# A recurrent attention kernel with streamed weights: 35 resident halves instead of 34, one shared work region, a new order of the step, and longer rows for streamed query and key halves

## The chip, the cores and the metric

The kernel runs on one core of a Trainium2 chip. The metric is the device time of one execution in microseconds, as the median of several runs. Engines are named as the profile names them: TensorE (PE; its weight loads are PEld), VectorE (DVE), ScalarE (ACT), GpSimd (POOL), and SyncE (SP), which here issues nearly all DMAs.

## The reference

The sequence has 2048 rows of 640 in bfloat16. Four residual sublayers follow one another: A, B, A, B, each on the layer norm of its input. Both layers use the same weights.

```python
# A: recurrent attention with a memory of 8 rows, 32 heads of 192, segments of 32 rows
for s in range(64):
    h = concatenate([mem, xs])                  # 8 + 32 rows
    q, k, v = h @ Wq, h @ Wk, h @ Wv            # each 640 x (32*192)
    p = softmax(where(mask, q @ k.T * scale, -1e9))
    o = (p @ v) @ Wo                            # (32*192) x 640
    mem, out_s = o[:8], o[8:]

# B: local attention, 32 heads of 20, each row sees 8 rows at distance 0, 2, ... 14 behind it
q, k, v = split(x @ wqkv)
o = softmax(q . k_window * scale) . v_window
out = o @ wo

x = x + A(layernorm(x)); x = x + B(layernorm(x))
x = x + A(layernorm(x)); x = x + B(layernorm(x))
```

The memory makes A a chain of 64 dependent segments. Its four weight matrices have 31.5 MB together, more than fits on the chip.

## The kernel before, in words

**Steps.** The kernel works in 67 steps, numbered 0 to 66. Step s runs A for segment s of layer 0 and for segment s - 2 of layer 1 (`LAG = 2`), stacked into one set of operands `ST` so that each weight is loaded once for both, and B for the segments that the step before finished. Step 66 has only B's part.

**Halves.** The four matrices of A are cut into 64 "halves" of 128 x 1920 elements (480 KB each): 0 to 31 are key and query halves (even and odd), 32 to 47 are V, 48 to 63 are output. 34 of them stay resident on the chip. The other 30 (`STREAMED`) come anew in every step, through a ring of five buffers `wt`. In step 0 a streamed half is loaded from the input and also written, in the layout of the ring, to a scratch tensor `Wr` in HBM; from step 1 on it comes from there, in two transfers of 240 KB (`half`). A ring buffer comes free when TensorE has done the last matmul of the half five places earlier.

**Order.** A hand-written list, `ORDER`, says in which order the parts of a step are issued. TensorE, VectorE, ScalarE and SP keep that order exactly; GpSimd's is chosen by the scheduler. The names that the text uses:

- q0 to q15: keys and queries of a pair of heads, 30 matmuls from two halves; ScalarE copies the result (`QK`). s0 to s3, exp0 to exp3, soft0 to soft3: scores of a group, their exponentials on ScalarE, and their normalisation on VectorE (`Pm`). t0 to t3: transposes of the probabilities, which VectorE copies to `PT`.
- va, vb, vc: the values of a group, copied to `V` by ScalarE, or by VectorE for what `V_ON_VECTOR` lists (two copies for each va or vb). pv0 to pv3: probabilities times values, copied by ScalarE to `ot`. o0 to o14: output projection, 15 matmuls from one half (o14 takes the last two), summed over the step in `acc`.
- sqr, stat, root, norm, qkv, prod, logits, explg, attn, e0 to e4, wo: layer norm and local attention of B. prod multiplies queries with the key window, layer 0 on VectorE and layer 1 on GpSimd; the latter is issued in qkv. e0 to e4 expand the weights on TensorE, and VectorE multiplies and sums them.
- sqx, statx, rootx, normx: layer norm of B's result, for layer 1's next segment. store: every fourth step, 128 finished rows are transposed, copied by ScalarE to `yo` and sent out from ScalarE's queue.
- xs, xr, xn, xt, xw: every fourth step, 128 new input rows are normalised (xs, xr, xn) and transposed (xt); xw transposes the rows themselves. alpha puts one segment of them into the next step's `ST`.

Before the change, the input rows `x_sb` are loaded at the head of each step with s % 4 = 1 (`input_load`), xs to xt run in the step after, and xw in the step with s % 4 = 0. `yo` and the normalised rows `xn` take turns in one buffer (tag `xn`). `prod`, `x_sb`, `xn`/`yo` and the layer norm's float32 scratch (tag `f32n`) have buffers of their own.

Of the kernel before, what the change touches and what calls it, by code (L numbers as in the profile page):

```python
# [10 lines left out]
BF16 = mybir.dt.bfloat16  # L11
F32 = mybir.dt.float32
ACT = mybir.ActivationFunctionType
ALU = mybir.AluOpType
# [8 lines left out]
P = 128  # L23
# [31 lines left out]
N_HALVES = 64  # L55
N_RESIDENT = 34
RING = 5


ORDER = """  # L60
q0 sqr0 q1 xs0 stat0 root0 xr0 q2 q3 q4 s0 exp0 norm0 va0 vb0 vc0 qkv0 q5 soft0 t0 q6 q7 prod0 pv0
va1 vb1 vc1 logits0 s1 explg0 exp1 o0 attn0 o1 q8 q9 q10 alpha0 o2 soft1 t1 e0 q11 q12 s2 e1 o3 exp2
e2 q13 q14 pv1 va2 vb2 vc2 soft2 e3 t2 q15 o4 e4 o5 s3 pv2 exp3 va3 soft3 vb3 vc3 o6 o7 wo0 t3 o8
xw0 xn0 o9 sqx0 o10 store0 pv3 o11 xt0 statx0 o12 o13 rootx0 normx0 o14
"""


def stages():
# [8 lines left out]
PLAN = stages()  # L77
V_ON_VECTOR = (("va", 1), ("vb", 1),)


STREAMED = (
    0, 3, 5, 6, 9, 11, 12, 13, 14, 16, 19, 21, 22, 24, 26, 29, 32, 35, 37, 41, 42, 46, 47, 48, 52, 53, 55, 57, 59,
    61,
)
# [11 lines left out]

def window1(ap, c):

    v = ap[:, c, :, 0:SEG]
    dims = [list(x) for x in v.ap]  # L100
    return bass.AP(v.tensor, v.offset, dims[:2] + [[BDIL, BW]] + dims[2:])
# [22 lines left out]
class Kernel:  # L124
# [21 lines left out]
    def constants(self):  # L146
# [10 lines left out]
        nc.vector.memset(self.zero, 0.0)  # L157
        m1 = self.w1.tile([P, LT], F32, name="mask1", tag="f32n")
        nc.gpsimd.memset(m1[:], 0.0)
        for u in range(2):  # L160
            r = slice(SLOT * u, SLOT * (u + 1))
            nc.gpsimd.affine_select(out=m1[r, :], in_=m1[r, :], compare_op=ALU.is_ge, fill=NEG, base=0,
                                    pattern=[[-1, LT]], channel_multiplier=1)
            nc.gpsimd.memset(m1[SLOT * u:SLOT * u + NM, :], 0.0)
        self.maskA = cp.tile([P, LT], BF16, name="maskA")
        nc.vector.tensor_copy(out=self.maskA[:, :], in_=m1[:, :])

        self.E = cp.tile([P, NCH, BH], BF16, name="E")
# [27 lines left out]
        self.wo = cp.tile([P, NCH, D], BF16, name="wo")  # L196

        self.kh = cp.tile([P, NCH, 2, BPAD + SEG], BF16, name="kh")
        self.vh = cp.tile([P, NCH, 2, BPAD + SEG], BF16, name="vh")
# [12 lines left out]
        nc.vector.tensor_reduce(out=self.maskL, in_=pairs, op=ALU.max, axis=AX.X)  # L212
        m_sb = self.w1.tile([NM, D], BF16, name="m_sb", tag="xn")
        nc.sync.dma_start(out=m_sb[:, :], in_=self.mem0)
        mt = self.ps.tile([P, NCH, NM], BF16, name="mt", tag="ps")
# [20 lines left out]
    def half(self, h):  # L236
        if h in self.resident:
            return self.resident[h]
        if h in RESIDENT:
            t = self.res.tile([P, HALF], BF16, name=f"res{h}")  # L240
            self.load_direct(t, h)
            self.resident[h] = t
            return t
        t = self.ring.tile([P, HALF], BF16, name="wt")
        if self.step == 0:
            self.load_direct(t, h)
            self.nc.gpsimd.dma_start(out=self.Wr[h][:, :], in_=t[:, :])
        else:
            for part in (slice(0, HALF // 2), slice(HALF // 2, HALF)):
                self.nc.sync.dma_start(out=t[:, part], in_=self.Wr[h][:, part])  # L250
        return t
# [7 lines left out]
    def input_load(self, t):  # L259
        self.x_sb = self.w1.tile([P, D], BF16, name="x_sb")  # L260
        self.nc.sync.dma_start(out=self.x_sb[:, :], in_=self.x[t * P:(t + 1) * P, :])

# [13 lines left out]
    def input_norm(self, t):  # L276
        nc = self.nc
        x_sb, st = self.x_sb, self.x_st
        nc.vector.scalar_tensor_tensor(out=st[:, 3:4], in0=st[:, 0:1], scalar=-1.0, in1=st[:, 2:3], op0=ALU.mult, op1=ALU.mult)
        xn = self.w1.tile([P, D], BF16, name="xn", tag="xn")  # L280
        nc.vector.tensor_scalar(out=xn[:, :], in0=x_sb[:, :], scalar1=st[:, 2:3], scalar2=st[:, 3:4], op0=ALU.mult, op1=ALU.add)
        self.x_n = xn

# [21 lines left out]
    def ln_square(self, src, n):  # L305
        nc = self.nc
        sq = self.w1.tile([P, NCH, n], F32, name="sq", tag="f32n")
        nc.gpsimd.tensor_tensor(out=sq[:, :, :], in0=src, in1=src, op=ALU.mult)
        ssq = self.w1.tile([P, n], F32, name="ssq", tag="ssq")
        nc.vector.tensor_reduce(out=ssq[:, :], in_=sq[:, :, :].rearrange("p c n -> p n c"), op=ALU.add, axis=AX.X)  # L310
        return ssq

    def ln_stats(self, src, ssq, n):
# [9 lines left out]
        nc.vector.scalar_tensor_tensor(out=r[:, :], in0=ps[:, 1, :], scalar=1.0 / D, in1=r[:, :], op0=ALU.mult, op1=ALU.subtract)  # L323
        xc = self.w1.tile([P, NCH, n], F32, name="xc", tag="f32n")
        nc.vector.tensor_tensor(out=xc[:, :, :], in0=src, in1=m[:, :].unsqueeze(1).to_broadcast([P, NCH, n]), op=ALU.subtract)
        return xc, r
# [163 lines left out]
    def b_square(self):  # L490
        self.ssq_b = self.ln_square(self.rows_of_b(), 2 * SEG)

    def b_stats(self):
        self.ln_b = self.ln_stats(self.rows_of_b(), self.ssq_b, 2 * SEG)
# [8 lines left out]
    def b_qkv(self):  # L503
# [13 lines left out]
        self.qT = qT  # L517
        self.prod = self.w1.tile([P, NCH, 2, BW, SEG], BF16, name="prod")
        self.products(1, nc.gpsimd)

# [4 lines left out]
    def b_logits(self):  # L525
# [3 lines left out]
        for c in range(NCH):  # L529
            for r in range(4):  # L530
                nc.tensor.matmul(ps[32 * r:32 * (r + 1), :, :], lhsT=self.E[:, c, :], rhs=self.prod[:, c, r // 2, :, hf * (r % 2):hf * (r % 2 + 1)],
                                 start=(c == 0), stop=(c == NCH - 1), tile_position=(0, 32 * r))
# [28 lines left out]
    def b_expand(self, c):  # L561
        nc = self.nc
        ps = self.ps.tile([P, 2, BW, SEG], F32, name="bc_ps", tag="ps")
        nc.tensor.matmul(ps[:, :, :, :].rearrange("p l w t -> p (l w t)"), lhsT=self.ET[:, c, :],  # L564
                         rhs=self.attn[:, :, :, :, :].rearrange("p l w h t -> p (l w h t)"), start=True, stop=True)
        pv = self.prod[:, c, :, :, :]
        nc.vector.tensor_tensor(out=pv, in0=ps[:, :, :, :], in1=window1(self.vh, c), op=ALU.mult)  # L567
        with nc.allow_low_precision("bf16 result of an f32 sum"):
            nc.vector.tensor_reduce(out=self.oT[:, c, :].rearrange("p (l t) -> p l t", l=2), in_=pv.rearrange("p l w t -> p l t w"), op=ALU.add, axis=AX.X)  # L569

    def b_wo(self):
        nc, s = self.nc, self.step
        ps = self.ps.tile([P, NCH, 2, SEG], F32, name="y_ps", tag="ps")
        for d in range(NCH):
            for c in range(NCH):
                nc.tensor.matmul(ps[:, d, :, :].rearrange("p l t -> p (l t)"), lhsT=self.wo[:, c, d * P:(d + 1) * P], rhs=self.oT[:, c, :],  # L576
                                 start=(c == 0), stop=(c == NCH - 1))
# [27 lines left out]
    def store(self):  # L605
        nc = self.nc
        k = self.step - 1 - LAG
        if k < 0 or k % 4 != 3:
            return
        ps = self.ps.tile([P, NCH, P], BF16, name="yt_ps", tag="ps")  # L610
        for c in range(NCH):
            nc.tensor.transpose(out=ps[:, c, :], in_=self.yT[:, c, :], identity=self.ident[:, :])
        yo = self.w1.tile([P, D], BF16, name="yo", tag="xn")
        nc.scalar.copy(out=yo[:, :], in_=ps[:, :, :].rearrange("p c d -> p (c d)"))
        nc.scalar.dma_start(out=self.out[(k // 4) * P:(k // 4 + 1) * P, :], in_=yo[:, :])


    def run(self):
# [5 lines left out]
        with tc.manual_schedule(engines={PE, SP, VECTOR, SCALAR}):  # L624
# [11 lines left out]
            local = {"sqr": self.b_square, "stat": self.b_stats, "root": self.b_root, "norm": self.b_norm, "qkv": self.b_qkv,  # L636
                     "prod": lambda: self.products(0, nc.vector), "logits": self.b_logits, "explg": self.b_exps, "attn": self.b_soft, "wo": self.b_wo,
                     "sqx": self.beta_square, "statx": self.beta_stats, "rootx": self.beta_root, "normx": self.beta_norm, "store": self.store}
            rows_in = {"xs": self.input_stats, "xr": self.input_root, "xn": self.input_norm, "xt": self.input_turn}
            for s in range(n_steps + 1):  # L640
# [7 lines left out]
                self.x2 = self.x2_next  # L648
                if s % 4 == 1 and 4 * (s // 4 + 1) < self.n_seg:
                    self.input_load(s // 4 + 1)  # L650
                for what, i in PLAN:
# [6 lines left out]
                    elif what == "alpha" and a and s + 1 < self.n_seg:  # L658
                        self.alpha_x(s + 1)
                    elif what in rows_in and s % 4 == 2 and 4 * (s // 4 + 1) < self.n_seg:  # L660
                        rows_in[what](s // 4 + 1)
# [59 lines left out]
```

## Time and profile before

| | |
|---|---|
| median of 3 runs | 3428.22 us (3424.91 to 3428.84) |
| the profiled execution | 3421.51 us, span 3419.7 us |
| TensorE, matmuls | 3225.9 us busy, 94% of the span |
| VectorE, ScalarE, GpSimd | 2323.2, 1969.7 and 338.5 us busy |
| DMA | 1025.24 MB, mean 300 GB/s |
| chain that ended last | PE 81%, DMA 11%, DVE 3% |

The span is the time from the first to the last instruction in the profiled execution. A busy TensorE is not TensorE at its peak, because the ends of matmuls are modelled and consecutive ones overlap; the distance between the starts of matmuls tells more. In the tables of waits each row names the engine and line that waited, what released it, the total in us, the number of times and the longest.

### The profile page before, as it was taken

The numbers are of one execution on the slowest core, as the hardware profiler recorded it, in microseconds if no ns is written. First come the engines' busy times: TensorE is split into PE (matmuls) and PEld (weight loads), VectorE is DVE, ScalarE is ACT, GpSimd is POOL, SyncE is SP. The second block draws the span as 40 slices with busy tenths as digits, with TensorE's granted clock in tenths as the row PEclk, the third lists the DMA queues.
The fourth block names the chain that finished last, engine by engine and source line by source line (L and its number), as shares of the span: only waits on it lengthen the run. The fifth ranks groups of instructions, "written<-read, shape, count | busy, mean of one in ns | idle before, by whom it ended". The sixth has DMA issues, their size and how long they took to land.

```text
span 3419.7 us, 184327 instructions
## 1 busy us (share of the span) xinstructions
PE 3225.9 (94%) x83325; PEld 2782.4 (81%) x83325; DVE 2323.2 (68%) x5322; ACT 1969.7 (58%) x4269; POOL 338.5 (10%) x456
## 2 busy tenths in 40 slices
PE   4799999999999999999999999999999999999997
PEld 3588888888888888888888888888888888888886
DVE  1367767766776766776677677767767766776775
ACT  1365665656555565565655556565565656556564
POOL 2101010000101001010100100100010010001000
PEclk7799999999999999999999999999999999999998
DMA  9999999998999989989988999998999989899995
GB/s 347 356 299 299 304 301 301 301 305 295 299 303 295 298 289 305 304 296 309 302 296 293 301 297 301 308 299 292 301 300 302 305 298 303 292 308 303 305 297 182
DMA packets 608612, 1025.24 MB, mean 300 GB/s; under 512 B 64456, under 2 KB 605264, under 8 KB 607824
## 3 DMA queue, kind: packets, MB, share of 16 engines
q1 hardware_dynamic: 603120, 996.08, 87.9%
q8 instruction: 651, 10.67, 1.3%
q0 software_dynamic: 2400, 14.75, 1.1%
q10 hardware_dynamic: 2304, 2.62, 0.2%
q14 instruction: 137, 1.12, 0.1%
HBM read 995.83 MB, written 17.37 MB: 296 GB/s over the span
## 4 chain that ended last, share of the span: by engine, by line
PE 81%; DMA 11%; DVE 3%; issue 2%; SPq 2%; ACT 1%; ACTq 0%; POOLq 0%; POOL 0%; DVEq 0%
PE qk_ps L345 26%; PE acc L458 15%; PE v_ps L409 12%; DMA wt<-Wr 8%; PE v_ps L428 7%; PE o_ps L441 4%; PE qkv_ps L514 3%; PE s_ps L357 3%; PE bc_ps L564 2%; PE s_ps L363 2%; PE qk_ps L340 1%; PE y_ps L576 1%; PE pt_ps L395 1%; SPq L250 1%; SPq L234 1%
## 5 line engine op out<-in xcount | busy, mean ns | idle before, releaser
L347 ACT CAST QK<-qk_ps 128x480 bf16<-128x480 f32 x1056 | 585.7, 560 | 648.6 <-PE qk_ps L345 481.6
L419 ACT CAST V<-v_ps 32x384 bf16<-32x384 f32 (+1 forms) x1848 | 849.7, 470 | 181.9 <-PE v_ps L428 128.4
L345 PE MATMUL qk_ps<-ST,wt 128*128 128x80 bf16 x14850 | 685.3, 203 | 49.8 <-DMA wt<-Wr 22.3
L345 PE MATMUL qk_ps<-ST,res 128*128 128x80 bf16 x14850 | 664.9, 203 | 20.8 <-issue 7.9
L345 PEld LDWEIGHTS <-wt 128*128 128x128 bf16 x14850 | 601.6, 101 | 79.4 <-DMA wt<-Wr 29.8
L345 PEld LDWEIGHTS <-res 128*128 128x128 bf16 x14850 | 590.2, 101 | 27.5 <-issue 13.2
L397 DVE TENSOR_SCALAR PT<-pt_ps,cf 128x320 bf16<-128x320 f32 x528 | 265.3, 544 | 274.4 <-PE pt_ps L395 274.4
L458 PE MATMUL acc<-ot,res 128*128 128x80 bf16 x8910 | 412.7, 203 | 32.0 <-ACT ot L444 19.8
L409 PE MATMUL v_ps<-res,ST 128*64 128x384 bf16 x2970 | 436.2, 329 | 6.7 <-DMA res<-in_A_Wv_dram 4.4
L458 PEld LDWEIGHTS <-res 128*128 128x128 bf16 x8910 | 364.6, 101 | 65.0 <-issue 51.3
L409 PEld LDWEIGHTS <-ST 128*64 128x64 bf16 x5280 | 289.9, 111 | 144.4 <-issue 45.4
L409 PE MATMUL v_ps<-wt,ST 128*64 128x384 bf16 x2310 | 380.7, 329 | 20.8 <-DMA wt<-in_A_Wv_dram 11.6
L569 DVE TENSOR_REDUCE oT<-prod 128x64 bf16<-128x512 bf16 x330 | 338.3, 1025 | 11.4
L458 PE MATMUL acc<-ot,wt 128*128 128x80 bf16 x6930 | 328.7, 203 | 8.1 <-DMA wt<-in_A_Wo_dram 4.3
L444 ACT CAST ot<-o_ps 128x480 bf16<-128x480 f32 x528 | 270.8, 566 | 96.3 <-PE o_ps L441 89.4
L374 ACT ACTIVATE sb<-sb 128x320 f32<-128x320 f32 x264 | 124.1, 470 | 350.3 <-DVE sb L370 350.3
L367 DVE TENSOR_TENSOR sb<-s_ps,maskA 128x320 f32<-128x320 f32 x264 | 128.3, 486 | 268.3 <-PE s_ps L363 268.2
L458 PEld LDWEIGHTS <-wt 128*128 128x128 bf16 x6930 | 279.0, 100 | 23.2 <-DMA wt<-in_A_Wo_dram 4.9
L567 DVE TENSOR_TENSOR prod<-bc_ps,vh 128x512 bf16<-128x512 f32 x330 | 225.2, 682 | 59.5 <-PE bc_ps L564 59.5
L428 PE MATMUL v_ps<-res,ST 128*32 128x384 bf16 x2970 | 265.5, 331 | 0.0
L428 PE MATMUL v_ps<-wt,ST 128*32 128x384 bf16 x2310 | 265.0, 331 | 0.4 <-issue 0.4
L522 POOL TENSOR_TENSOR prod<-qT,kh 128x1280 bf16<-128x1280 bf16 x66 | 163.1, 2472 | 817.3 <-ACT kh L516 817.3
(119 smaller groups left out, 3911.1 us busy)
## 6 DMA issues: line engine op xcount, KB each, us to landing
wt<-Wr SPq DMA_DIRECT2D x3900, 240.0 KB, 4.8
Wr<-wt POOLq DMA_DIRECT2D x30, 480.0 KB, 6.4
res<-in_A_Wv_dram SPq DMA_DIRECT2D x9, 480.0 KB, 10.8
res<-in_A_Wo_dram SPq DMA_DIRECT2D x9, 480.0 KB, 11.1
wt<-in_A_Wk_dram SPq DMA_DIRECT2D x8, 480.0 KB, 10.0
res<-in_A_Wq_dram SPq DMA_DIRECT2D x8, 480.0 KB, 11.1
res<-in_A_Wk_dram SPq DMA_DIRECT2D x8, 480.0 KB, 10.2
wt<-in_A_Wq_dram SPq DMA_DIRECT2D x8, 480.0 KB, 9.7
```

The source lines that it names most:

```text
L345: nc.tensor.matmul(ps[:, m, :, :], lhsT=w[m // 3][:, c, (m % 3) * P:(m % 3 + 1) * P], rhs=st[:, c, PAD:WIDE], start=(c == 0), stop=(c == N ...
L347: nc.scalar.copy(out=self.QK[i % NQK][:, 0:12 * LT].rearrange("p (m l t) -> p m l t", m=6, l=2), in_=ps[:, :, :, :].rearrange("p m t l -> ...
L397: nc.vector.tensor_scalar(out=self.PT[:, :, :, l, :], in0=ps[:, :, :, :], scalar1=self.maskL[:, l:l + 1], scalar2=None, op0=ALU.mult)
L409: nc.tensor.matmul(ps[r:r + 64, :], lhsT=st[:, c, MID:WIDE], rhs=self.wv[j][:, c, :], start=(c == 0), stop=(c == NCH - 1), tile_position=( ...
L419: self.nc.scalar.copy(out=out, in_=in_)
L428: nc.tensor.matmul(ps[r:r + 32, :], lhsT=st[:, c, 0:MID], rhs=self.wv[j][:, c, :], start=(c == 0), stop=(c == NCH - 1), tile_position=(0, ...
L441: nc.tensor.matmul(ps[64 * slot:64 * (slot + 1), jj, n, :, :], lhsT=self.V[:, i % 4, col:col + 64], rhs=self.PT[:, i % 4, h, :, :], start= ...
L444: nc.scalar.copy(out=ot[:, :, :, :], in_=ps[:, :, :, :, :].rearrange("p j n l t -> p (j n) l t"))
L458: nc.tensor.matmul(a[:, at, :, :], lhsT=w[h][:, m, dc * P:(dc + 1) * P], rhs=self.ots[h // 2][:, 3 * (h % 2) + m, :, :], start=(h == 0 and ...
L522: engine.tensor_tensor(out=self.prod[:, :, l, :, :], in0=self.qT[:, :, l, :].unsqueeze(2).to_broadcast([P, NCH, BW, SEG]), in1=window(self ...
L567: nc.vector.tensor_tensor(out=pv, in0=ps[:, :, :, :], in1=window1(self.vh, c), op=ALU.mult)
L569: nc.vector.tensor_reduce(out=self.oT[:, c, :].rearrange("p (l t) -> p l t", l=2), in_=pv.rearrange("p l w t -> p l t w"), op=ALU.add, axi ...
```

## The change

One more half is resident: 35 instead of 34, so 29 are streamed in each step, and the list of streamed halves is a new one (17 key and query halves, 4 of V and 8 output halves; before 16, 7 and 7). The room comes from one shared tile `work` of 128 x 2560: `prod` uses all of it, and at other times of the step `x_sb`, the float32 scratch, `x_n` and `yo` use one quarter of it each. A streamed key or query half comes from `Wr` in one transfer with rows of 3,840 bytes; V and output halves come in two transfers with rows of 1,920 bytes as before. ORDER is new. The input rows are loaded at the end of the step (ld) when s % 4 is 2, and once more when s % 4 is 3, since `prod` overwrites them in between; xs to xt run in the step with s % 4 = 3. VectorE copies va0, va1 and va2 instead of va1 and vb1. After segment 63, B works on layer 1 alone: prod of layer 1 goes to VectorE, prod of layer 0 is left out, and the expansion and projection cover half the columns.

```diff
-N_RESIDENT = 34
+N_RESIDENT = 35
...
-q0 sqr0 q1 xs0 stat0 root0 xr0 q2 q3 q4 s0 exp0 norm0 va0 vb0 vc0 qkv0 q5 soft0 t0 q6 q7 prod0 pv0
-va1 vb1 vc1 logits0 s1 explg0 exp1 o0 attn0 o1 q8 q9 q10 alpha0 o2 soft1 t1 e0 q11 q12 s2 e1 o3 exp2
-e2 q13 q14 pv1 va2 vb2 vc2 soft2 e3 t2 q15 o4 e4 o5 s3 pv2 exp3 va3 soft3 vb3 vc3 o6 o7 wo0 t3 o8
-xw0 xn0 o9 sqx0 o10 store0 pv3 o11 xt0 statx0 o12 o13 rootx0 normx0 o14
+xs0 q0 q1 sqr0 xr0 stat0 q2 root0 q3 q4 xn0 xw0 s0 va0 vb0 norm0 vc0 exp0 q5 q6 xt0 qkv0 soft0 prod0
+q7 t0 q8 s1 pv0 exp1 va1 vb1 vc1 logits0 o0 q9 explg0 q10 soft1 q11 attn0 t1 o1 o2 e0 q12 s2 exp2
+pv1 va2 vb2 vc2 soft2 e1 o3 o4 e2 q13 e3 q14 t2 q15 o5 e4 s3 pv2 alpha0 va3 exp3 vb3 wo0 o6 vc3
+soft3 o7 store0 sqx0 o8 t3 statx0 o9 o10 pv3 o11 rootx0 o12 o13 o14 ld0 normx0
...
-V_ON_VECTOR = (("va", 1), ("vb", 1),)
+V_ON_VECTOR = (("va", 0), ("va", 1), ("va", 2),)
...
-    0, 3, 5, 6, 9, 11, 12, 13, 14, 16, 19, 21, 22, 24, 26, 29, 32, 35, 37, 41, 42, 46, 47, 48, 52, 53, 55, 57, 59,
-    61,
+    3, 4, 7, 9, 10, 12, 13, 14, 15, 17, 19, 22, 24, 25, 27, 29, 31, 34, 39, 40, 47, 48, 51, 53, 54, 55, 56, 57,
+    60,
...
+        self.work = cp.tile([P, 4 * D], BF16, name="work")
+        self.prod = self.work[:, :].rearrange("p (c l w t) -> p c l w t", c=NCH, l=2, w=BW)
+        self.x_sb = self.work[:, 0:D]
+        self.f32n = self.work[:, D:2 * D].bitcast(F32)
+        self.x_n = self.work[:, 2 * D:3 * D]
+        self.yo = self.work[:, 3 * D:4 * D]
...
-            for part in (slice(0, HALF // 2), slice(HALF // 2, HALF)):
+            for part in (slice(0, HALF),) if h < 32 else (slice(0, HALF // 2), slice(HALF // 2, HALF)):
                 self.nc.sync.dma_start(out=t[:, part], in_=self.Wr[h][:, part])
...
+    def layers(self):
+
+        return (0, 1) if self.step <= self.n_seg else (1,)
...
-        self.prod = self.w1.tile([P, NCH, 2, BW, SEG], BF16, name="prod")
-        self.products(1, nc.gpsimd)
+        self.products(1, nc.gpsimd if self.step <= self.n_seg else nc.vector)
...
-        yo = self.w1.tile([P, D], BF16, name="yo", tag="xn")
-        nc.scalar.copy(out=yo[:, :], in_=ps[:, :, :].rearrange("p c d -> p (c d)"))
-        nc.scalar.dma_start(out=self.out[(k // 4) * P:(k // 4 + 1) * P, :], in_=yo[:, :])
+        nc.scalar.copy(out=self.yo, in_=ps[:, :, :].rearrange("p c d -> p (c d)"))
+        nc.scalar.dma_start(out=self.out[(k // 4) * P:(k // 4 + 1) * P, :], in_=self.yo)
...
-                if s % 4 == 1 and 4 * (s // 4 + 1) < self.n_seg:
-                    self.input_load(s // 4 + 1)
...
-                    elif what in rows_in and s % 4 == 2 and 4 * (s // 4 + 1) < self.n_seg:
+                    elif what == "ld" and s % 4 in (2, 3) and 4 * (s // 4 + 1) < self.n_seg:
+                        self.input_load(s // 4 + 1)
+                    elif what in rows_in and s % 4 == 3 and 4 * (s // 4 + 1) < self.n_seg:
                         rows_in[what](s // 4 + 1)
```

In `b_expand` and `b_wo` the layer index becomes a slice `ls = slice(self.layers()[0], 2)`, with no other change there. The mask `maskA` is built in the scratch quarter of `work`, later among the constants.

## The prediction, as it was put on record before the changed kernel ran

> **What bounds the kernel now.** I read the page first, then who waited for whom on TensorE, then the waits of SP's queue, then the timeline around two stalls.
>
> ```profile
> PE 3225.9 (94%) x83325; PEld 2782.4 (81%) x83325; DVE 2323.2 (68%) x5322; ACT 1969.7 (58%) x4269; POOL 338.5 (10%) x456
> ...
> q1 hardware_dynamic: 603120, 996.08, 87.9%
> q8 instruction: 651, 10.67, 1.3%
> ...
> wt<-Wr SPq DMA_DIRECT2D x3900, 240.0 KB, 4.8
> ```
>
> TensorE leads and the DMA engines are nearly as full. From the trace, a step is the time from one step's first matmul of q0 (L340) to the next one's. Steps 3 to 63 average 50.0 us; adding each plan item's unstalled spacing gives 47.0. So about 3 us of each step are stalls, some 180 us in all, and that is what can be won. By step number modulo 4 the means are 49.22, 50.81, 50.87 and 49.08: kinds 1 and 2 are about 1.7 us longer. Waits of TensorE:
>
> ```profile
> PE qk_ps L345 <- issue: 23.3, 44, 1.6
> PE qk_ps L345 <- DMA wt<-Wr: 22.3, 42, 2.0
> PE acc L458 <- ACT ot L444: 19.8, 15, 1.4
> ```
>
> Columns: total us, times, longest. Late weights, late `ot` in exactly 15 places, and "issue". Measuring each matmul's start against its usual distance from the one before (this also sees stalls hidden in the modelled ends), steps 3 to 63 hold 52.6 us of waits for wt<-Wr, 22.7 for `ot`, 70 of "issue", 10 of all else named. The DMA waits are 29.9 us in kind-1 steps and 7.5 in each other kind; the `ot` waits are all in kind 2. SP's waits say why for kind 1:
>
> ```profile
> SPq L250 <- DMA wt<-Wr: 71.7, 221, 1.1
> ...
> SPq L261 <- PE tp L295: 26.0, 14, 2.1
> ```
>
> At the head of kind-1 steps SP wants to reload x_sb, which TensorE still has to transpose at the old step's end (xw0). For about 2 us every ring load behind it stands. Then q1 and q3 find their weights missing (20 of the 29.9 us). For kind 2, the timeline at a step's end:
>
> ```profile
> 1840.08 0.69 ACT L614 COPY yo<-yt_ps 128x640 bf16<-128x640 bf16 x1 [2.06 <-PE tp L295]
> 1840.80 0.34 ACTq L615 DMA_DIRECT2D out_dram<-yo  x1
> 1841.18 1.02 ACT L444 CAST ot<-o_ps 128x480 bf16<-128x480 f32 x2 [0.41 <-ACT yo L614]
> ```
> ```profile
> 1841.79 0.70 PE L458 MATMUL acc<-ot,res 128*128 128x80 bf16 x15 [1.40 <-ACT ot L444]
> ```
>
> yo and xn share a buffer, so yo's copy waits until xt0 has transposed xn, and the `ot` copies that o12 needs stand behind yo. The "issue" stalls lie 128 matmuls apart: 256 instructions, one of the 651 packets of 10.67 MB on DMA queue q8. They end about 1.4 us after such a packet has come: they are instruction fetches. The packet starts a median 1.8 us after the block before it began, takes 1.0, and a block runs 4.6 to 5.4 us.
>
> **The change, part by part.** The instructions of TensorE are the same in number. All prices below are against the profiled execution, 3421.5 us (span 3419.7); the median of the runs is 6.7 higher.
>
> (1) ld0 stands at the step's end, behind o12's load. Its x region was last read by the expansion, which wo0 needs too, long before SP gets there. Kind 1 loses its extra DMA waits: 29.9 - 7.6 = **-22**. The second load of x per four steps is 160 KB, 0.5 us of queue at 300 GB/s, in a place where no slot is free anyway: 0; without that cover 16 x 0.5 = 8.
>
> (2) The store moves ahead of sqx0, over 3 us before pv3, yo has a place of its own, and xt0 and xw0 move to where ACT holds no `ot`: **-22** (at least 19.8 by the row).
>
> (3) Other waits for weights, 30 us now. Per step 29 halves instead of 30. Packets of 1,920 B take 79 ns at the median, the 640 of 3,840 B (wqkv) 149. Per step 30 x 256 x 79 / 16 = 37.9 us of each DMA engine become 17 x 128 x 149 / 16 + 12 x 256 x 79 / 16 = 35.4. A merged half is also issued once (428 ns) instead of twice, and with 41 DMAs for 60 a queue slot (the 71.7 us row) stops holding issues back. Against that stands the new order. A half's lead is TensorE's time from the end of the half five streamed before it to its own use. Item spacings from the trace: q 1.08, qkv 2.25, s 0.62, va 0.82, t 0.15, stat 0.40. Before, vb0's half 35 has stat, three q, s and va: 5.1 us; it lands a median 0.25 too late. After, the shortest is q8's half 17: q6, qkv, q7, t0 = 4.56. One 240-KB transfer lands 3.7 us after issue with two others out, 4.4 with four; the second half of a merged one adds 0.62 (the landing interval of a full queue): 4.3 or 5.0. Few loads are released just before it, so mostly 4.3, and half 17 costs something in a third of the steps. Ends: -30 and, were it always 5.0, +28 on top of no gain. I take 10 us left, **-20**.
>
> (4) Last step: only layer 1 is computed. TensorE waited 2.05 us for POOL's product; VectorE's alone ends 2.3 earlier. The five expansions take 1.63 us each; from L325 (481 ns at 320 elements, 314 at 160) and L310 (713 and 421) half a width saves about 0.73 each, 3.7: **-6**.
>
> (5) One half less is written to Wr in step 0: 0.49 MB at 355 GB/s, **-1.4**.
>
> (6) Stalls removed let TensorE reach the next instruction block sooner. The fetches have a median 0.8 us to spare; of 64 us I let a fifth come back: **+12** (ends 0 and 25).
>
> (7) VectorE takes two more V copies of 0.555 us, ACT two fewer of 0.47. From t1's PT to wo0's sums VectorE then has 16.0 us of back-to-back work beside 15.5 of TensorE's (t1's end to wo0's end), and pv2's PT comes up to 0.42 late. Stalls of TensorE in that stretch absorb most: **+6** (ends 0 and 64 x 0.42 = 27).
>
> (8) prod0 moves ahead of t0's PT, which pv0 needs. Two pairs of rows, POOL first, then VectorE first (last step):
>
> ```profile
> 1704.33 2.46 POOL L522 TENSOR_TENSOR prod<-qT,kh 128x1280 bf16<-128x1280 bf16 x1 [11.76 <-ACT kh L516]
> ```
> ```profile
> 1704.85 2.62 DVE L522 TENSOR_TENSOR prod<-qT,kh 128x1280 bf16<-128x1280 bf16 x1
> ```
> ```profile
> 3398.08 0.83 DVE L522 TENSOR_TENSOR prod<-qT,kh 128x1280 bf16<-128x1280 bf16 x1 [3.02 <-ACT kh L516]
> 3398.12 3.09 POOL L522 TENSOR_TENSOR prod<-qT,kh 128x1280 bf16<-128x1280 bf16 x1 [6.31 <-ACT kh L516]
> ```
>
> The one that starts second loses the other's time. After the change VectorE reaches prod0 about 0.3 us before kh is copied (exp0 frees both: soft0 takes 1.35, q5, q6, qT and kh on ACT 1.66), so it goes first: 0.83 us, PT in time, price **0**. If POOL goes first, PT ends 0.55 us late: 64 x 0.55 = 35. The Trainium skill, "SBUF — State Buffer", section "Who interferes with whom", says that issue order, not the shape of the operation, decides who of VectorE and GpSimd blocks; both pairs of rows agree, and by it the price is 0 or 35 and nothing between.
>
> The moved root0, norm0, exp0, alpha0 and normx0 keep over 0.4 us to their users by the same spacings: 0. POOL's order stays, its product becomes 0.6 longer, and logits0 comes 3 us after it.
>
> Sum: -22 - 22 - 20 - 6 - 1.4 + 12 + 6 = -53.4. 3421.5 - 53.4 = 3368.1; on the median, 3428.2 - 53.4 = **3374.8**.
>
> **Rivals.** (A) Instruction fetches wait longer, and it gets slower. A fetch packet started 0.8 us after its block with two transfers out, 1.2 with four, 2.2 with six, and 2.8 in step 0 (768 and 1,280-B rows, transfers of 480 KB). If it must wait behind one transfer's eight rows per engine, that goes from 8 x 79 = 0.63 us to 8 x 149 = 1.19. Shifting every fetch of the trace later by 0.3 us adds 33 us of stalls, by 0.56 it adds 93; from about 0.4 on, the gain is gone. At 0.56: 3428 - 53 + 93 = 3468. For it: step 0. Against: the wait grows with the number of transfers out, which falls from 60 to 41 a step. The Trainium skill, "DMA: Bandwidth & Descriptors", section "Queues, rings and completion order", has each engine drain a whole packet of several descriptors from one ring before it turns to the next; by that the wait would follow the merged size, and the growth with depth in the trace speaks against that as the whole story. Chance 0.11.
>
> (B) POOL goes first at prod0 and pv2's PT is late as well: +35 + 21 on the sum, 3431. Against it: the 0.3 us. Chance 0.07.
>
> (C) The freed time comes back at fetches and at q8's weights: half of (1) to (3) lost, 3428 - 20 = 3408. Chance 0.10.
>
> That the merged transfer is still cut into small packets I rule out: wqkv's rows of 3,840 B went as such.
>
> **How the numbers follow.** Forecast 0.72, C 0.10, B 0.07, A 0.11. Measurement tells 0.2% (7 us) from no change. Faster: 0.72 + 0.10 = 0.82; B lies at the edge, 0.05 same and 0.02 slower; slower 0.11 + 0.02 = 0.13. Low end: no wait left in (3), (6) and (7) nothing, fetches 25 us shorter by the smaller depth: 3428 - 22 - 22 - 30 - 7 - 25 = 3322, so 3320. High end: B with a few us of A, 3440; most of A is left out.
>
> **What would show it.** Right: SP's wait for tp and TensorE's for `ot` gone; all four kinds of step within 0.5 us of each other, near 49; VectorE's product at 0.8 to 0.9 us and POOL's near 3.1; "issue" near 55 us in the waits of TensorE. Wrong: a new TensorE wait for wt at plan item q8, for PT at pv0 or pv2, or "issue" above 100.

## The result

| | before | after |
|---|---|---|
| median | 3426.56 us (3423.32 to 3428.84, 4 runs) | 3461.22 us (3459.74 to 3472.96, 4 runs) |
| ratio to before, 95% interval | | 1.0109 [1.0085, 1.0133] |
| profiled span | 3419.7 us | 3457.8 us |

The change makes the kernel 1.1% slower; 3374.8 was forecast, and 3461 lies above the range. From the page of the changed kernel, engines, DMA queues and transfers:

```profile
PE 3207.9 (93%) x83325; PEld 2768.4 (80%) x83325; DVE 2284.2 (66%) x5454; ACT 1930.7 (56%) x4137; POOL 368.6 (11%) x453
...
q1 hardware_dynamic: 427440, 966.52, 83.3%
q8 instruction: 651, 10.67, 1.2%
...
wt<-Wr SPq DMA_DIRECT2D x1105, 480.0 KB, 5.3
wt<-Wr SPq DMA_DIRECT2D x1560, 240.0 KB, 4.7
```

The weight queue q1 is less full (83.3% for 87.9%), as the sum said. TensorE, VectorE and ScalarE are all a little less busy than before. TensorE's waits (total us, times, longest):

```profile
PE qk_ps L349 <- issue: 71.8, 81, 3.1
PE o_ps L445 <- DVE PT L401: 21.9, 54, 0.5
PE o_ps L445 <- issue: 18.7, 23, 1.5
```

The two rows of before for late weights and late `ot` have gone from the top. In their place stands a threefold "issue" on the key and query line (71.8 for 23.3, longest 3.1 for 1.6), and PT at pv, 54 times. Three measures are used from here on, all over steps 3 to 63 of a trace. "Issue" is the sum of matmul delays over 250 ns against the usual distance, where nothing that the trace names was late; waits with a name (weights, `ot`, PT) count from some 50 ns on. "Boundary" is the sum of delays over 100 ns at the first matmul of each of the 602 instruction blocks of 128 matmuls. "Fetch start" is the time from a block's first matmul to the start of the next instruction packet on queue q8. A transfer is "out" from its issue until it has landed, which is the last update of its semaphore before that semaphore is used again.

The account of steps 3 to 63, before to after: issue 69.8 to 168.6 (+98.8), weights 52.6 to 9.2 (-43.4), `ot` 22.7 to 1.1 (-21.6), PT 0 to 29.1 (+29.1), other named waits +3, the rest of the matmul spacing -20; sum +46. Steps 0 to 2 add -0.1 together and steps 64 to 66 -7.9: +38, as the spans differ by 38.1. So all that was to be won was won, and the instruction fetches took more than that back.

### The profile page after: what moved, and what is told of

Same layout as the page of the kernel before. It is cut to its first block, busy times and chain, and to the rows that moved or that the text cites. A ratio compares the mean times of both kernels' runs of the same rounds, so it can differ in the third digit from the quotient of the medians.

```text
span 3457.8 us, 183004 instructions
## 1 busy us (share of the span) xinstructions
PE 3207.9 (93%) x83325; PEld 2768.4 (80%) x83325; DVE 2284.2 (66%) x5454; ACT 1930.7 (56%) x4137; POOL 368.6 (11%) x453
## 3 DMA queue, kind: packets, MB, share of 16 engines
q1 hardware_dynamic: 427440, 966.52, 83.3%
## 4 chain that ended last, share of the span: by engine, by line
PE 68%; DVE 19%; DMA 6%; issue 5%; SPq 1%; ACT 1%; POOLq 0%; ACTq 0%; DVEq 0%
PE qk_ps L349 22%; PE acc L462 13%; PE v_ps L413 10%; DVE oT L577 6%; PE v_ps L432 5%; DVE work L575 4%; PE qkv_ps L522 4%; PE o_ps L445 3%; DMA wt<-Wr 3%; DVE PT L401 2%; PE qk_ps L344 2%; PE s_ps L361 2%; DVE V L421 2%; PE s_ps L367 2%; PE y_ps L585 2%
## 5 line engine op out<-in xcount | busy, mean ns | idle before, releaser
L349 PE MATMUL qk_ps<-ST,wt 128*128 128x80 bf16 x16830 | 772.1, 203 | 58.7 <-issue 37.3
L349 PEld LDWEIGHTS <-wt 128*128 128x128 bf16 x16830 | 676.2, 101 | 97.9 <-issue 65.2
L349 PE MATMUL qk_ps<-ST,res 128*128 128x80 bf16 x12870 | 595.0, 203 | 45.8 <-issue 34.5
L349 PEld LDWEIGHTS <-res 128*128 128x128 bf16 x12870 | 522.5, 100 | 68.6 <-issue 41.6
L462 PE MATMUL acc<-ot,res 128*128 128x80 bf16 x7920 | 345.8, 203 | 13.7 <-DMA res<-in_A_Wo_dram 7.1
L462 PEld LDWEIGHTS <-wt 128*128 128x128 bf16 x7920 | 322.6, 101 | 42.7 <-issue 24.2
L577 DVE TENSOR_REDUCE oT<-work 128x64 bf16<-128x512 bf16 (+1 forms) x330 | 334.2, 1013 | 11.4
L462 PEld LDWEIGHTS <-res 128*128 128x128 bf16 x7920 | 307.4, 101 | 20.1 <-DMA res<-in_A_Wo_dram 8.1
L529 POOL TENSOR_TENSOR work<-qT,kh 128x1280 bf16<-128x1280 bf16 x64 | 198.3, 3099 | 669.8 <-ACT kh L524 669.8
L413 PE MATMUL v_ps<-wt,ST 128*64 128x384 bf16 x1320 | 263.4, 330 | 6.0 <-DMA wt<-in_A_Wv_dram 4.4
L421 DVE CAST V<-v_ps 64x384 bf16<-64x384 f32 x396 | 218.6, 552 | 29.3 <-PE v_ps L413 25.1
L575 DVE TENSOR_TENSOR work<-bc_ps,vh 128x512 bf16<-128x512 f32 (+1 forms) x330 | 223.1, 676 | 7.8 <-PE bc_ps L572 5.4
```

The source lines that it names most:

```text
L349: nc.tensor.matmul(ps[:, m, :, :], lhsT=w[m // 3][:, c, (m % 3) * P:(m % 3 + 1) * P], rhs=st[:, c, PAD:WIDE], start=(c == 0), stop=(c == N ...
L413: nc.tensor.matmul(ps[r:r + 64, :], lhsT=st[:, c, MID:WIDE], rhs=self.wv[j][:, c, :], start=(c == 0), stop=(c == NCH - 1), tile_position=( ...
L421: self.nc.vector.tensor_copy(out=out, in_=in_)
L462: nc.tensor.matmul(a[:, at, :, :], lhsT=w[h][:, m, dc * P:(dc + 1) * P], rhs=self.ots[h // 2][:, 3 * (h % 2) + m, :, :], start=(h == 0 and ...
L529: engine.tensor_tensor(out=self.prod[:, :, l, :, :], in0=self.qT[:, :, l, :].unsqueeze(2).to_broadcast([P, NCH, BW, SEG]), in1=window(self ...
L575: nc.vector.tensor_tensor(out=pv, in0=ps[:, ls, :, :], in1=window1(self.vh, c, ls), op=ALU.mult)
```

## The experiments

The theory after the result (T, later T1) was the prediction's rival A: an instruction packet waits behind what one DMA engine still has to move of the weight transfer in front of it, and merging two transfers doubles that. Its rivals: the new order stalls by itself (a fetch falls at a worse place), the longer row of 3,840 B is at fault, or more bytes are out at a time. In the expectations R is the first of these, and T2 stands first for the row and in the runs with four buffers for the bytes. All measures in one table, one execution each, times as medians, ratios to runs of the kernel before made beside them:

| kernel | us | ratio [95%] | fetch start, median / 90th percentile, ns | boundary us | issue us | weights us | PT us |
|---|---|---|---|---|---|---|---|
| before | 3426.6 | | 1904 / 2812 | 83 | 70 | 53 | 0 |
| after | 3461.2 | 1.0109 [1.0085, 1.0133] | 2166 / 3399 | 185 | 169 | 9 | 29 |
| e1_split | 3382.7 | 0.9866 [0.9840, 0.9891] | 1924 / 2866 | 102 | 83 | 20 | 32 |
| e2_before_merged | 3522.1 | 1.0289 [1.0253, 1.0325] | 2038 / 3391 | 176 | 155 | 41 | 0 |
| e3_long_rows | 3986.2 | 1.1643 [1.1600, 1.1686] | 2430 / 4841 | 364 | 412 | 243 | 11 |
| e4_all_merged | 3515.0 | 1.0258 [1.0210, 1.0306] | 2085 / 3604 | 237 | 235 | 7 | 26 |
| e5_split_t2 | 3361.9 | 0.9811 [0.9783, 0.9839] | 2013 / 2926 | 101 | 83 | 27 | 0 |
| e6_one_short | 3455.5 | 1.0080 [1.0051, 1.0108] | 2140 / 3320 | 177 | 162 | 10 | 31 |
| e7_two_long | 3456.2 | 1.0098 [1.0066, 1.0130] | 1938 / 3005 | 123 | 119 | 51 | 26 |
| e8_three | 3615.7 | 1.0556 [1.0525, 1.0587] | 1254 / 1972 | 21 | 5 | 333 | 0 |
| e9_ring4 | 3594.6 | 1.0500 [1.0449, 1.0551] | 1891 / 3287 | 126 | 111 | 218 | 7 |
| e10_split_ring4 | 3575.8 | 1.0427 [1.0383, 1.0471] | 1696 / 2764 | 56 | 46 | 252 | 3 |

The granted clock of TensorE in the profiled executions lies between 0.980 and 0.986, but for 0.977 in e4_all_merged and 0.956 in e3_long_rows. In these two the spacing outside of the stalls is longer as well, by some 20 and 110 us against the changed kernel.

**The merge alone, from both sides.** e1_split is the changed kernel with all halves in two transfers:

```diff
-            for part in (slice(0, HALF),) if h < 32 else (slice(0, HALF // 2), slice(HALF // 2, HALF)):
+            for part in (slice(0, HALF // 2), slice(HALF // 2, HALF)):
```

> The changed kernel with every streamed half in two transfers of 1,920-byte rows again; order, residents and shared region stay as changed. Theory T (an instruction fetch waits behind one engine's share of a weight transfer, and merging doubled that share): the instruction-fetch stalls at block boundaries, 185 us in steps 3 to 63 of the changed kernel and 83 in the one before, fall back to 80 to 95, and the time to 3350 to 3380 us. Rival R (the new order, or the vanished weight waits, expose the fetches whatever the transfers are): fetch stalls stay at 160 to 185 and the time within 20 us of 3461. Both: the wait of pv2 for PT stays, about 29 us.

Its waits of TensorE:

```profile
PE qk_ps L349 <- issue: 26.8, 46, 1.5
PE o_ps L445 <- DVE PT L401: 23.8, 59, 0.5
```

One edit takes the "issue" row from 71.8 to 26.8 and the time from 3461 to 3383; PT stays. Boundary stalls (102 us) and time came out a little above what T said. e2_before_merged is the reverse edit in the kernel before, all else as it was.

> The kernel before with one edit: its streamed query and key halves come in one transfer of 3,840-byte rows. T: fetch stalls rise from 83 us to 160 to 190 although order and residents are the old ones, the other DMA waits fall by 10 to 30, and the time rises to 3470 to 3510 us. R: fetch stalls stay near 83, and the time is 3400 to 3430 us.

```profile
PE qk_ps L345 <- issue: 63.5, 77, 2.4
PE acc L458 <- issue: 28.1, 28, 1.8
PE acc L458 <- ACT ot L444: 19.8, 15, 1.4
```

In the old order the merge does the same: issue 70 to 155, time +2.9% (3522 us, 12 above T's range), while `ot` keeps its 15 waits. In both orders it adds 85 us of issue (168.6 - 83.3, 155.1 - 69.8) and saves 11 to 12 us of weight waits. That rules out the new order as the cause.

**More merging, and less.** e4_all_merged merges V and output halves too, `for part in (slice(0, HALF),):`.

> The changed kernel with the V and output halves in one transfer too (29 transfers a step for 41). T: the blocks that run in the V and output stretches lose what those in the query stretches lost, fetch stalls rise from 185 to 230 to 280 us, the time to 3500 to 3560 us. R: fetch stalls stay at 165 to 200 us, the time within 20 us of 3461.

```profile
PE qk_ps L349 <- issue: 71.1, 71, 3.2
PE o_ps L445 <- issue: 39.6, 26, 3.6
```

Issue goes on rising, 169 to 235, where weights have nothing left to give (7 us). e8_three goes the other way: the kernel of e5_split_t2 (below) with each half in three transfers of 160 KB, `for part in (slice(0, 640), slice(640, 1280), slice(1280, HALF)):`.

> The split kernel with t2 moved, and every streamed half in three transfers of 1,280-byte rows (87 a step). T1 and T2 both: the fetch meets shares of 8 x 55 = 0.44 us, fetch stalls fall under 75 us. Against it: at most eight transfers are out, 2.7 halves instead of 4, and SP issues 87 x 0.43 = 37 us a step, so the waits for weights rise from 20 to 50 or more. I expect 3350 to 3400 us, the second weighing more than the first.

```profile
PE qk_ps L349 <- DMA wt<-Wr: 109.3, 309, 1.9
PE acc L462 <- DMA wt<-Wr: 64.9, 99, 2.2
```

The fetch stalls are nearly gone (issue 5 us, fetch start 1254 ns at the median), but weights now cost 333 us. The time was expected at 3350 to 3400 us and is 3616. In no trace are more than eight weight transfers out at once, so with smaller ones fewer bytes are under way: a mean of 1139 KB at the block starts, against 1427 in e1_split. SP's 87 issues of 0.43 us also take 37 of the 53 us of a step; which of the two weighs more was not tested. Of the three sizes, two transfers a half is the best.

**Is it the row or the transfer?** e3_long_rows keeps the rows of 3,840 B, but loads a query or key half in two transfers of 64 neighbouring partitions:

```diff
+                for rows_ in (slice(0, P // 2), slice(P // 2, P)):
+                    self.nc.sync.dma_start(out=t[rows_, :], in_=self.Wr[h][rows_, :])
```

> The changed kernel with each streamed query or key half in two transfers of 64 partitions with 3,840-byte rows: the rows stay long, a transfer has 240 KB. T with the transfer's share as the measure (4 rows x 149 ns = 0.60 us per engine beside 8 x 79 = 0.63 split and 8 x 149 = 1.19 merged): fetch stalls fall to 80 to 100 us and the time to 3350 to 3385 us, as with two transfers of short rows. T with the single row as the measure (149 instead of 79 ns): fetch stalls stay at 160 to 185 us and the time near 3461. R: as the changed kernel.

It could not answer: it is limited by something else. Its page:

```profile
DMA packets 450534, 995.30 MB, mean 248 GB/s; under 512 B 62600, under 2 KB 305808, under 8 KB 449744
...
q1 hardware_dynamic: 445120, 966.59, 93.2%
```

A packet of 3,840 B took 260 ns at the median instead of 149, so the queue is full with fewer GB/s. e7_two_long takes the even and the odd partitions instead, `t[k::2, :]` from `self.Wr[h][k::2, :]` for k in 0 and 1, and packets are back at 149 ns.

> The changed kernel with each streamed query or key half in two transfers, of the even and of the odd partitions, rows of 3,840 bytes. T1: an engine's share of a transfer is 4 x 149 = 0.60 us, fetch stalls 80 to 110 us, time 3370 to 3400 us, provided that rows of 3,840 bytes keep their 149 ns (on 64 neighbouring partitions they took 260). T2: fetch stalls 150 to 190 us, time 3440 to 3490 us. If the packets again take over 200 ns, the run tells only about the partitions.

```profile
PE qk_ps L353 <- DMA wt<-Wr: 38.1, 54, 1.8
PE qk_ps L353 <- issue: 31.2, 42, 2.4
```

Fetch start returns to 1938 / 3005, near the 1924 / 2866 of e1_split, with the long rows in place. Nor were fewer bytes out: a mean of 1399 KB at the block starts, against 1427 in e1_split. But boundary stalls (123 us) lie between what T1 and T2 said, weights come later (51 us), and the time, 3456, is where T2 had it; why the time is not won was not settled. So this run leans to T1 and does not decide. e6_one_short is the counterpart: one transfer of 480 KB made of 256 rows of 1,920 B (`Wr` is laid out as `[2, P, HALF // 2]` for key and query halves, and one DMA reads both).

> The changed kernel with each streamed query or key half in one transfer, but of 256 rows of 1,920 bytes (the scratch tensor in HBM holds the two column halves apart). Theory T1 (the fetch waits behind an engine's share of one transfer, 16 x 79 = 1.26 us here): fetch stalls stay at 160 to 200 us and the time at 3440 to 3490 us. Theory T2 (it waits by the length of a single row, or of a fixed number of rows: 79 ns each as in the split kernel): fetch stalls 80 to 110 us, time 3370 to 3400 us. T1 also holds if what counts is the deeper queue that fewer transfers allow.

```profile
PE qk_ps L355 <- issue: 68.9, 84, 2.4
PE o_ps L451 <- DVE PT L407: 23.1, 57, 0.5
```

With the short rows of before, and one transfer, all is as in the changed kernel: 3320 ns, issue 162, 1.0080. The row's length is not the cause. What is left is the transfer's size, or the bytes out that grow with it.

**Share of a transfer, or bytes out?** Merged halves also let more bytes be out at once: in e1_split no block began with more than 1,920 KB out, after the change 57 of 602 did. Taking only blocks that began with 1,400 to 1,700 KB out, the 90th percentile of the fetch start was 2842 ns before, 2952 in e1_split, 3180 after, 3227 in e2_before_merged and 3137 in e4_all_merged; with 1,900 to 1,930 KB out it was 3214, 3289, 3501, 3967 and 3894. The merged kernels wait longer at equal bytes. To set the limit equal, e9_ring4 is the changed kernel and e10_split_ring4 is e1_split, both with `RING = 4` for 5.

> The changed kernel with four ring buffers instead of five, so that at most 4 halves (1,920 KB) can be out at once, as many as the kernels with 240-KB transfers ever have (8 transfers). This parts the two readings that are left of why the fetch packets come later with merged transfers. Theory T1 (a fetch waits behind an engine's share of one transfer, 8 rows of 3,840 B = 8 x 149 ns = 1.19 us): the start of the fetch packet after its block keeps its 90th percentile above 3.2 us (changed kernel 3.40, all in two transfers 2.87), and stalls at block boundaries stay above 140 us (185 and 102). Rival T2 (it waits because more bytes are out, up to 5 halves): the 90th percentile falls to about 2.9 us and the boundary stalls to about 100 us. Both expect more waits for weights than the 9 us of the changed kernel, since each half is asked for one place later: 60 to 200 us, so slower than 3461 us under T1 (3480 to 3600), 3430 to 3530 under T2.

> The changed kernel with every half in two transfers of 240 KB and with four ring buffers instead of five: the pair to the run with merged transfers and four buffers, at the same limit of bytes out. T1 (share of one transfer): the 90th percentile of the fetch packet's start is 0.4 to 0.6 us below that of the pair, at 2.9 us or less, and the boundary stalls are at least 50 us below. T2 (bytes out): both within 0.2 us and 25 us of the pair. Waits for weights 60 to 200 us in both; time 3430 to 3520 us.

The waits of e9_ring4 and then of e10_split_ring4:

```profile
PE acc L462 <- DMA wt<-Wr: 87.2, 169, 1.9
PE qk_ps L349 <- DMA wt<-Wr: 80.9, 124, 2.4
PE qk_ps L349 <- issue: 36.5, 46, 3.2
```
```profile
PE qk_ps L349 <- DMA wt<-Wr: 91.9, 179, 2.4
PE acc L462 <- DMA wt<-Wr: 84.8, 167, 1.8
...
PE qk_ps L349 <- issue: 11.9, 27, 1.3
```

The difference in fetch start stays: 3287 against 2764, 0.52 us, with a mean of 1353 KB out at the block starts against 1265, and boundary stalls are 70 us apart. Going from five buffers to four takes only 0.1 us from the 90th percentile of either kernel. So of the difference between merged and split, the share of a transfer makes most and the bytes out little. Within one kernel the wait still grows with what is out: before, the median was 1148 ns with four transfers out and 2400 with eight; after, 2252 with four. Some expectations were missed: e9_ring4 has 126 us of boundary stalls, where T1 said over 140, both kernels wait over 200 us for weights, where 60 to 200 was expected, and e10_split_ring4 is slower than forecast, 3576 for 3430 to 3520. That TensorE's waits for weights give the fetches time, which would explain the 126, was not tested.

**PT at pv2.** e5_split_t2 is e1_split with t2 two places earlier, ahead of e3, so that VectorE copies its PT before the last two expansions:

```diff
-... e2 q13 e3 q14 t2 q15 o5 ...
+... e2 q13 t2 e3 q14 q15 o5 ...
```

> All streamed halves in two transfers (as in the split kernel, 3383 us), and t2 moved in the order from behind q14 to behind q13, ahead of e3, so that VectorE copies PT of group 2 before it sums e3. Theory P (VectorE's 16 us of back-to-back work from t1's PT to wo0 makes PT late for pv2): the waits of pv2 for PT, 32 us in the split kernel, fall under 8, and the time goes to 3345 to 3365 us. Rival: the same work is only passed on, e3 and e4 come later and wo0 or s3 waits instead; time within 10 us of 3383.

```profile
PE qk_ps L349 <- issue: 25.2, 49, 1.3
...
PE qk_ps L349 <- DMA wt<-Wr: 12.2, 29, 1.0
```

The row of PT is gone from the waits, 32 us of it, and the median falls by 20.9 us to 3361.9 (3346.9 to 3369.4). Part comes back: weights 20 to 27. This version beats both kernels: 0.9811 [0.9783, 0.9839] of the time of before.

## Why the prediction was wrong, step by step

**The step that failed is the weight of rival A.** Its mechanism and its price were in the text: a fetch waits behind one transfer's eight rows per engine, 0.63 us to 1.19, and a shift of 0.56 adds 93 us of stalls, 3468 in all. Measured: the 90th percentile of the fetch start moved by 0.59 us (e1_split to after 0.53), the merge added 85 us, and the time is 3461. It was given 0.11 on one argument: the wait grows with the number of transfers out, and that number falls. So the sum held only term (6), +12, for the fetches, and measured +98.8. The number did fall, at the block starts from a mean of 6.02 to 4.40. But each transfer now weighs more: the bytes out went from 1446 KB to 1515, and at equal bytes the fetches still came later, so a fall in number bought nothing. Step 0, the only place of the trace with transfers of 480 KB, spoke for A with 2.8 us and was set aside. That A's 3468 comes within 7 us of the result is partly luck: its price moved every fetch by 0.56 us, while the median moved by 0.26, and the 23 us that PT cost above its price are nearly made up by the -20 of the rest.

The Trainium skill, "DMA: Bandwidth & Descriptors", section "Queues, rings and completion order", has an engine drain a packet of some 9 to 17 descriptors from one ring before it turns to the next. By that the wait follows the merged size and not the row, which is what e6_one_short (16 short rows per engine) and the pair with four buffers show. The Trainium skill, "Runtime: NRT & Kernel Launch", section "Instruction fetch mechanics", calls the crossing of a 256-instruction block mostly hidden. Here 70 us before and 169 after were not hidden, 0.12 and 0.28 us for each of the 602 blocks of some 5 us: little for one block, and more in sum than all that the change won.

**The other steps.** (1) and (3): 42 us forecast, 43.4 measured; SP's wait of the input load for tp is gone, and half 17 at q8, the shortest lead, was late in 12 of 61 steps, 4.1 us in all. Split transfers get 32.5 of it. (2): -22 forecast, -21.6. (4): -6 forecast, -5.5 from step 65's last matmul to the end. (5): -1.4 forecast, -1.5. (6), the time given back at the fetches: +12 forecast, +13.5 in e1_split, where the merge doesn't hide it.

(7) was mis-sized: 6 us forecast with 27 as the upper end, 29 to 32 measured. VectorE's instructions in one step of the changed kernel, then TensorE's:

```profile
1701.72 1.03 DVE L577 TENSOR_REDUCE oT<-work 128x64 bf16<-128x512 bf16 x1
1702.67 1.00 DVE L401 TENSOR_SCALAR PT<-pt_ps,cf 128x320 bf16<-128x320 f32 x2
```
```profile
1700.68 0.31 PE L399 MATMUL pt_ps<-ident,Pm 128*128 128x80 bf16 x4
...
1703.72 0.62 PE L445 MATMUL o_ps<-PT,V 128*64 128x80 bf16 x24 [0.25 <-DVE PT L401]
```

t2's transposes were done at 1701.0, but VectorE came to the copy at 1702.67, behind the expansion, and pv2 waited. On the page that is 21.9 us in 54 waits, 0.41 each: the 0.42 of the working was right. What failed is "stalls of TensorE in that stretch absorb most"; nearly every step waits. e5_split_t2 takes the wait away by an order alone.

(8) came out as priced, VectorE first in all 64 steps:

```profile
1728.09 0.82 DVE L529 TENSOR_TENSOR work<-qT,kh 128x1280 bf16<-128x1280 bf16 x1 [0.43 <-ACT kh L524]
```
```profile
1728.13 3.10 POOL L529 TENSOR_TENSOR work<-qT,kh 128x1280 bf16<-128x1280 bf16 x1 [12.42 <-ACT kh L524]
```

Not forecast: outside of the stalls counted here, the spacing is some 20 us smaller in four kernels of the new order (after, e1_split, e5_split_t2, e6_one_short), and not in e2_before_merged. It lies in short delays: when all delays over 50 ns are counted, 2864 us are left before and 2872 after. Before, 45 us are in delays of 50 to 250 ns, over half of them "issue" on the matmuls of the values (va, vb, vc); after, it is 15. Why the values were delayed less was not settled. Without the merge and with t2 moved, the forecast of 3375 is passed: 3362.

The four kinds of step were to lie within 0.5 us near 49. They lie from 50.19 to 50.99 after, and from 48.69 to 49.50 in e5_split_t2.

## What to carry to other kernels

A long unrolled program fetches its instructions by DMA beside its data, and here a bigger data transfer made the fetches wait longer: where "issue" stalls come at a fixed number of instructions, price a transfer's size by the wait it puts before the next fetch, and try it both ways. Splitting has its own limit, since the number of transfers out was bounded (eight here): 160 KB starved the ring, 480 KB starved the fetches, and 240 KB was best. When an argument goes by how much is out, count it in bytes and not in transfers, and price the share of one transfer by itself.

## What the runs showed of the hardware that was not expected

The choice of partitions changes a packet's time: rows of 3,840 B to 64 neighbouring partitions took a median of 260 ns a packet (quartiles 227 and 282) and the kernel fell to 248 GB/s, while the same rows to every second partition, or to all 128, took 149. The Trainium skill, "DMA: Bandwidth & Descriptors", section "The descriptor swizzle", puts, in its example of 128 partitions, partitions 0 to 63 on the even write ports and 64 to 127 on the odd ones; a transfer of one half would then use half of the ports, which these packet times agree with, though no run here tells ports apart.
